# Chunked attention and four gated attention experts: turned weights of two pairs interlaced, outputs in a ring, and a new order of the steps

## The chip, the cores and the metric

The kernel runs on one core of a Trainium2 chip. The metric is the device time of one execution in microseconds (us); less is better. The cores' engines are named as the profile names them: PE (TensorE matmuls, PEld their weight loads), DVE (VectorE), ACT (ScalarE), POOL (GpSimd), SP (SyncE, which issues nearly all DMAs).

## What is computed

For 8 batches of 8 heads, 576 positions and 64 values a head: attention within chunks of 64 positions, whose output is the input x of four attention experts with a causal softmax over all 576 positions, gated by the top two of four logits.

```python
scores = np.matmul(q_c, k_c.transpose(0, 1, 2, 4, 3)) / 8      # chunks of 64
attn = np.exp(scores - scores.max(-1, keepdims=True))
attn = attn / (attn.sum(-1, keepdims=True) + 1e-09)
x = np.matmul(attn, v_c)                                       # then (B, S, H * D)
logits = x @ w_gate                                            # top 2 of E=4, softmax -> w
for e in range(E):
    q, k, v = x @ wq[e], x @ wk[e], x @ wv[e]                  # 512 -> 64
    s = np.where(causal, -1e9, q @ k.T / 8)
    a = softmax(s)
    out += mask[..., None] * w[:, :, kk:kk + 1] * (a @ v @ wo[e])
```

## The kernel before

All matmuls are float32; the projections, the expert scores and the output projection are made from three products of a high and a low half (hi·hi, hi·lo, lo·hi). The 4608 rows of x are 36 groups of 128. The work of PE is cut into 372 **steps**, in this text and in the table `ORDER` by their names:

- `as` u (L510): chunk scores of unit u (one or two groups; the first four units, 0 to 3, are one group each). DVE takes the maxima and subtracts them (L520, L522), ACT makes the exponentials (L529), DVE sums and reciprocals (L531, L533, L535), DVE (group 0) or POOL (all others) multiplies by them (L538).
- `at` u (L549): the chunk weights are turned on PE, and copied from PSUM into the tile `et` (ACT L557, and DVE L554 for half of units 0 and 1, which `FAST` names). `av` u (L570): chunk values, which ACT and DVE split into `xh` and `xl` (L592, L594).
- `m` i and `v` g (both L461, in `project`): queries and keys of a column tile, and the values and gate logits of a group. ACT and DVE split the results (L627, L632, L634; `vv` L490).
- `s` p (L712): causal scores of pair p (one batch, two experts), six steps a pair (p.1 to p.5 and p) of 64 to 448 columns, two banks each, one bank for each of the two experts. DVE evicts each bank with the mask and the row minimum (L722), ACT makes exponentials and sums (L729), POOL multiplies by reciprocal and gate (L753).
- `st` (L786): the expert weights are turned, four steps a pair; ACT copies them into the tile `aT` (L800), DVE adds three corners (L764). `o` p (L820): weights times values for the pair, read from two `aT` tiles, one for each expert; ACT and DVE split them into `uh` and `ul` (L829, L834). `w` i (L850): output projection of 128 rows, copied out by ACT or DVE (L861, L864) and stored.

The weights come in as eight transfers of 256 or 260 KB (L439), are rounded by ACT (L442) and their low halves made by POOL (L446).

The steps use PE in four **forms**: quarters of the array (`as`, `av`), halves by rows (`at`, `st`, `s`), halves by columns (`o`), and the full array (`m`, `v`, `w`).

The order on PE is the hand-written table `ORDER`. A list scheduler (`Plan`), run when the program is built, follows it with its own table of costs, and from its clock the order on the other engines results; `LATER` and `MOVED` shift their keys, `LOADS` orders the first DMAs, and `FILLS` puts idle matmuls (L892) between the first steps. A step holds tiles from pools: 8 PSUM banks (`bank`), `e` and `et` tiles for the chunk weights, two `aT` tiles, four `at` tiles of raw expert weights. A step can't be placed before every tile in its `uses` is free.

## Time and profile before

| | us |
|---|---|
| median of 3 runs | 386.6 (386.0 to 387.44) |
| the profiled execution | 386.02 |
| its span in the profile | 384.3 |
| PE busy | 374.5 (97%) |
| DVE, ACT, POOL busy | 272.1, 270.3, 170.7 |

The profile has one execution, cut by engine, by source line and by tile. PE's matmuls are pipelined and their ends are modelled, so that neighbouring rows overlap; what a step costs is read from the distance of its start to the next one's.

### The profile page before, as it was taken

How to read it: one execution, taken by the hardware profiler on the slowest of the kernel's cores; microseconds unless marked ns; L12 is line 12 of the kernel's file. 1: busy time of each engine (PE TensorE's matmuls, PEld its weight loads, DVE VectorE, ACT ScalarE, POOL GpSimd, SP SyncE). 2: the span in 40 equal slices, each digit the busy share in tenths (PEclk: the TensorE clock that was granted, in tenths of full speed). 3: DMA queues.
4: the chain of work that ended last, by engine and by line, in shares of the span. 5: the costliest groups of instructions: out<-in, count | busy, mean ns of one | idle time of the engine just before them, and what ended most of it. 6: DMA issues, size and time to landing. Idle time of an engine off the chain costs nothing.

```text
span 384.3 us, 14186 instructions
## 1 busy us (share of the span) xinstructions
PE 374.5 (97%) x5602; PEld 330.2 (86%) x5603; DVE 272.1 (71%) x946; ACT 270.3 (70%) x890; POOL 170.7 (44%) x335
## 2 busy tenths in 40 slices
PE   6799999999999999999999999999999999999996
PEld 4699999898989899797997989988989889897674
DVE  3667899999489795888436779776755766668531
ACT  3564799789746965979744496798494765969651
POOL 6653255657163069455160205763705046166700
PEclk9999999999999999999999999999999999999999
DMA  8954532605252270414106126003100110000224
GB/s 286 380 200 181 195 96 78 217 3 148 77 184 93 90 245 28 163 61 139 57 29 197 53 68 239 29 3 128 67 17 15 30 58 1 2 29 3 110 84 164
DMA packets 22098, 40.76 MB, mean 106 GB/s; under 512 B 2448, under 2 KB 2704, under 8 KB 22032
## 3 DMA queue, kind: packets, MB, share of 16 engines
q1 hardware_dynamic: 21744, 39.47, 29.8%
q8 instruction: 44, 0.72, 0.8%
q10 hardware_dynamic: 288, 0.39, 0.3%
q14 instruction: 22, 0.18, 0.1%
HBM read 30.42 MB, written 9.44 MB: 104 GB/s over the span
## 4 chain that ended last, share of the span: by engine, by line
PE 92%; DMA 3%; DVE 2%; ACT 1%; issue 1%; POOL 1%; SPq 0%; POOLq 0%
PE bank L461 39%; PE bank L850 14%; PE bank L820 12%; PE bank L712 11%; PE bank L786 6%; PE bank L570 5%; PE bank L510 4%; PE bank L549 2%; DMA at<-in_wqk_dram 2%; DMA qs<-in_qt_dram 1%; POOL e L538 1%; DVE xl L594 0%; DVE e L522 0%; DVE mx L520 0%; ACT e L529 0%
## 5 line engine op out<-in xcount | busy, mean ns | idle before, releaser
L753 POOL TENSOR_SCALAR at<-at,st,gate 128x320 f32<-128x320 f32 (+4 forms) x160 | 95.0, 611 | 74.5 <-DVE st L743 49.0
L729 ACT ACTIVATE at<-at,st 128x448 f32<-128x448 f32 (+4 forms) x160 | 90.0, 601 | 0.1
L722 DVE CUSTOM_DVE_ANT_0 at<-bank,mask 128x448 f32<-128x448 f32 (+4 forms) x160 | 60.0, 425 | 12.2 <-PE bank L712 11.4
L461 PE MATMUL bank<-xh,wqk_hi 128*128 128x384 f32 (+1 forms) x208 | 65.5, 326 | 0.0
L461 PE MATMUL bank<-xl,wqk_hi 128*128 128x384 f32 (+1 forms) x208 | 65.2, 323 | 0.0
L461 PE MATMUL bank<-xh,wqk_lo 128*128 128x384 f32 (+1 forms) x208 | 65.1, 323 | 0.0
L800 ACT ACTIVATE aT<-bank 128x128 f32<-128x128 f32 (+2 forms) x256 | 57.0, 377 | 2.4 <-PE bank L786 2.0
L538 POOL TENSOR_TENSOR e<-e,mx 128x1024 f32<-128x1024 f32 (+1 forms) x21 | 34.3, 1645 | 50.1 <-DVE mx L535 28.3
L820 PE MATMUL bank<-aT,vv 128*64 128x448 f32 (+4 forms) x384 | 46.7, 392 | 0.0
L820 PEld LDWEIGHTS bank<-aT,vv 128*64 128x64 f32 x384 | 25.0, 137 | 21.8 <-issue 15.2
L764 DVE STREAM_TRANSPOSE aT<-at 32x96 f32<-32x96 f32 x128 | 34.5, 269 | 12.5 <-POOL at L753 9.0
L461 PE MATMUL bank<-wvg_hi,xh 128*128 128x260 f32 x144 | 40.5, 288 | 0.0
L461 PE MATMUL bank<-wvg_lo,xh 128*128 128x260 f32 x144 | 39.7, 283 | 0.0
L461 PE MATMUL bank<-wvg_hi,xl 128*128 128x260 f32 x144 | 39.5, 281 | 0.0
L461 PEld LDWEIGHTS bank<-xh,wqk_hi 128*128 128x128 f32 x208 | 38.2, 188 | 0.8
L461 PEld LDWEIGHTS bank<-xl,wqk_hi 128*128 128x128 f32 x208 | 38.4, 188 | 0.5 <-DVE xl L594 0.2
L461 PEld LDWEIGHTS bank<-xh,wqk_lo 128*128 128x128 f32 x208 | 38.3, 188 | 0.0
L729 ACT ACTIVATION_READ_ACCUMULATOR at<-at,st 128x1 f32 (+1 forms) x160 | 38.1, 239 | 0.0
L712 PE MATMUL bank<-kh,qh 64*128 64x288 f32 (+4 forms) x192 | 37.1, 338 | 0.0
L490 ACT ACTIVATE vv<-bank 64x260 f32<-64x260 f32 (+1 forms) x56 | 21.6, 385 | 22.0 <-PE bank L461 21.6
L712 PE MATMUL bank<-kl,qh 64*128 64x288 f32 (+4 forms) x192 | 32.8, 294 | 0.0
L786 PEld LDWEIGHTS bank<-ident,at 64*128 64x128 f32 x704 | 28.9, 139 | 3.8 <-issue 1.5
(91 smaller groups left out, 822.4 us busy)
## 6 DMA issues: line engine op xcount, KB each, us to landing
ks<-in_kt_dram SPq DMA_DIRECT2D x36, 256.0 KB, 4.7
vs<-in_vt_dram SPq DMA_DIRECT2D x36, 256.0 KB, 4.1
qs<-in_qt_dram SPq DMA_DIRECT2D x35, 256.0 KB, 5.0
out_dram<-y SPq DMA_DIRECT2D x35, 256.0 KB, 2.0
at<-in_wqk_dram SPq DMA_DIRECT2D x4, 256.0 KB, 6.4
at<-in_wvg_dram SPq DMA_DIRECT2D x2, 260.0 KB, 4.3
at<-in_wo_dram SPq DMA_DIRECT2D x2, 256.0 KB, 5.7
qs<-in_qt_dram ACTq DMA_DIRECT2D x1, 256.0 KB, 3.6
```

The source lines that it names most:

```text
L461: pe.matmul(bk.t[:, :n_], a, x, start=(n == 0), stop=(n == 3 * KT - 1))
L490: act.activation(v_s[b].t[p0:p0 + m, j], bk.t[r0:r0 + m, 0:W_VG], AF.Copy)
L538: o = add("DVE" if u in NORM_DVE else "Pool", 0.6 if u in NORM_DVE else 0.14 + 0.87 * G, lambda: norm.tensor_tensor(e.t[:, al], e.t[:, al] ...
L712: pe.matmul(bks[s].t[:m, :w], q[own, cs], k[own, z0 + ks.start:z0 + ks.stop], start=(x == 0), stop=(x == 2))
L722: dve.tensor_tensor_reduce(out=a.t[:r, o_ + ks.start:o_ + ks.stop], in0=bk.t[:r, :w], in1=mask[:r, m0:m0 + w], scale=1.0, scalar=first, op ...
L729: act.activation(af, af, AF.Exp, scale=-1.0, bias=st.t[:r, 0, i, 0:1], accum_out=st.t[:r, 1, i, 0:1])
L753: pool.tensor_scalar(af, af, st.t[:r, 2, i, 0:1], gt.t[:r, i, e:e + 1], op0=OP.mult, op1=OP.mult)
L764: dve.transpose(dst, src)
L786: pe.transpose(bks[r].t[:, 64 * n:64 * n + 64], a.t[own, c0:c0 + 128], ident[own, own])
L800: act.activation(dst, bks[r].t[:, n:n + 64 * m].rearrange("p (j c) -> p j c", j=m), AF.Copy)
L820: pe.matmul(bk.t[64 * s:64 * s + 64, c0 - h0:h1 - h0], vs.t[:, j, 64 * (2 * pair + s):64 * (2 * pair + s) + 64], ts[s].t[:, 448 * j + c0:4 ...
L850: pe.matmul(bk.t, up[:, k, 128 * t:128 * t + 128], wp[:, k, :], start=(n == 0), stop=(n == 5))
```

## The change

- **Turned weights.** The `aT` tiles grow from 2368 to 3392 columns, and the two experts of a pair lie interlaced in one tile (`place`, with an offset table `A_OFF` for each). Two tiles so hold two pairs, where they held one.
- **Chunk weights** are turned in place: the `et` tiles are gone, `at`'s result is copied back into `e`, of which there are now three.
- **Outputs** `uh`, `ul` are a ring of 768 columns instead of 1152; where a piece wraps it is split into two (ACT 732 instructions in its order become 738, DVE 881 become 893).
- **Claims.** A step on PE claims banks (and its operands) alone; the tiles its results go to are claimed by the copies behind it. The wait of a projection for the scores that read the old queries and keys moves from the step to ACT's copy.
- **Groups 0 and 1.** The exponentials go back into the PSUM banks, DVE sums there, and DVE multiplies in two halves from PSUM into `e` (L541, L553 of the changed kernel). POOL's part in group 1 is gone.
- New planner costs, a list `EARLY` that fixes the first entries of DVE and ACT, another order of the first loads, one idle matmul between `as0` and `as1` instead of two and two new ones before `av0`, and a new `ORDER` of the same 372 steps, with new `LATER` and `MOVED`.

```diff
-TT = 448 * 4 + S
+TT = 2816 + S
-ZW = 768
+ZW = UW = 768
-A_OFF = (640, 0, 256, 768, 1280)
+A_OFF = ((640, 0, 256, 768, 1280), (1472, 1600, 1152, 576, 0))
+RAW = (768, 0)
+def place(s, j, q):
+
+    return 2816 - 576 * j + q if s else 448 * j + q
...
 ORDER = """
-as0 as1 at0 at1 av0 as3 av1 as2 v0 m1 m0 v0.1 m2 m3 v1 m3.1 m0.1 v1.1 m2.1 m1.1 at3 at2 as4 av3 av2 as5 v3 v2 m4 m6
+as0 as1 at0 at1 av0 av1 as3 m3 m0 v0 m0.1 m2 m2.1 as2 m1 m3.1 m1.1 v0.1 at3 s1.1 s0 s1 s0.1 at2 as4 av3 av2 as5 v1
...
-FILLS = {("as", 1): 2, ("at", 0): 9}
+FILLS = {("as", 1): 1, ("at", 0): 9, ("av", 0): 2}
...
-LOADS = [(x[:2], int(x[2:])) for x in "lq0 lw4 lw5 lq1 lv0 lw0 lw2 lv1 lw1 lw3 lq2 lv2 lq3 lv3 lq4 lv4".split()]
+LOADS = [(x[:2], int(x[2:])) for x in "lq0 lq1 lw4 lv0 lw5 lw0 lv1 lw2 lw1 lw3 lq2 lv2 lq3 lv3 lq4 lv4".split()]
+EARLY = [x + "@DVE" for x in ("ad0 ad0.1 ad0.2 ad0.3 ad0.4 ad0.5 ad0.6 ad0.7 ap0 ap0.1 ad1 ad1.1 ad1.2 ad1.3 ac0 ad1.4 ay0 ay0.1 ad1.5 "
+                              "ad1.6 ad1.7 ap1 ap1.1 ac1 ay1 ay1.1").split()]
+EARLY += [x + "@ACT" for x in "aa0 aa0.1 wh4 ac0 aa1 aa1.1 ax0 ax0.1 wh5 ac1 ax1 ax1.1 wh0 wh2 wh1 wh3".split()]
...
-    e_p = tiles(2, [128, 2 * H, 64], "e")
-    et_p = tiles(2, [128, 2, 512], "et")
+    e_p = tiles(3, [128, 2 * H, 64], "e")
...
-    a_p = tiles(4, [128, 1856], "at")
-    t_p = tiles(2, [128, TT], "aT")
+    a_p = [tiles(2, [128, 1856], f"at{s}") for s in range(2)]
+    t_x = tiles(2, [128, TT], "aT")
+    t_p = [list(t_x), list(t_x)]
...
-    uh = sb.tile([128, 2, 2 * S], F32R, name="uh")
+    uh = sb.tile([128, 2, UW], F32R, name="uh")
...
+        if u in FAST:
+            for s, hs in enumerate(halves):
+                o = add("ACT", act_t(64 * nh, sbuf=True), lambda s=s, hs=hs: act.activation(
+                    ps(s), e.t[:, hs], AF.Exp, scale=0.125), deps=od[s:s + 1], uses=[bq[s], e], name=("aa", u))
+                os.append(add("DVE", dve_t(64 * nh), lambda s=s, hs=hs: dve.tensor_reduce(
+                    mx.t[:, 1, hs, 0], ps(s), axis=AX.X, op=OP.add), deps=[o], uses=[bq[s], mx], name=("ad", u)))
...
+        if u in FAST:
+            od = [add("DVE", dve_t(64 * nh), lambda s=s, hs=hs: dve.tensor_tensor(
+                e.t[:, hs], ps(s), mx.t[:, 3, hs, 0:1].to_broadcast([128, nh, 64]), op=OP.mult),
+                deps=[o], uses=[bq[s], e, mx], name=("ap", u)) for s, hs in enumerate(halves)]
...
-                    et.t[:, c, 0:64 * nh], b2[c].t[:, 0:64 * nh], AF.Copy),
-                    deps=[o], uses=[b2[c], et], name=("ac", u)))
+                    et()[:, c, 0:64 * nh], b2[c].t[:, 0:64 * nh], AF.Copy),
+                    deps=[o], uses=[b2[c], e], name=("ac", u)))
...
-                po = add("PE", SCORES[w], f, deps=need, uses=bks + both, name=("s", bp), form="rows", n_ins=12.2)
+                po = add("PE", SCORES[w], f, deps=need, uses=bks, name=("s", bp), form="rows", n_ins=12.2)
...
-        o = add("PE", TURNS[half], f, deps=deps, uses=[a, t, t_s[b, e ^ 1]] + bks,
+        o = add("PE", TURNS[half], f, deps=deps, uses=[a] + bks,
...
-                                  ts[s].t[:, 448 * j + c0:448 * j + h1], start=(j == 0), stop=(j == js[-1]),
+                                  ts[s].t[:, place(s, j, c0):place(s, j, h1)], start=(j == 0), stop=(j == js[-1]),
...
+            c = (S * b + h0) % UW
+            w = min(h1 - h0, UW - c)
+            for c, p0, w in ((c, 0, w), (0, w, h1 - h0 - w))[:1 + (w < h1 - h0)]:
```

The new `ORDER` moves three things that the prediction speaks of. First PE, where the values steps stand. Before, `o3` stands alone between chunk values and a projection (the two experts' tiles are aT_105 and aT_106, and the banks are written by both in turn):

```order
L570 MATMUL bank_63<-et_84,vs_79 64x64 x2
L820 MATMUL bank_68<-aT_105,vv_99 64x128
L820 MATMUL bank_68<-aT_106,vv_99 64x128
L820 MATMUL bank_66<-aT_105,vv_99 64x448
...
L820 MATMUL bank_66<-aT_106,vv_99 64x64
L461 MATMUL bank_62<-xh_88,wqk_hi 128x384
```

In the changed kernel `o1` and `o0`, the values of two pairs (tiles aT_105 and aT_104), stand back to back:

```order
L592 MATMUL bank_67<-e_82,vs_79 64x64 x2
L838 MATMUL bank_64<-aT_105,vv_98 64x128 x2
L838 MATMUL bank_61<-aT_105,vv_98 64x448 x4
...
L838 MATMUL bank_61<-aT_105,vv_98 64x64 x2
L838 MATMUL bank_65<-aT_104,vv_98 64x128 x2
L838 MATMUL bank_66<-aT_104,vv_98 64x448 x4
...
L838 MATMUL bank_66<-aT_104,vv_98 64x64 x2
L731 MATMUL bank_63<-kh_95,qh_91 72x64
```

All sixteen values steps stand in such pairs now. Second ACT, its first entries (bank numbers with the pool's own behind them; `[waits ...]` are the semaphores of an instruction). Before:

```order
L442 ACT_TABLE_LOAD
L442 ACTIVATE wvg_hi_160<-at0_101 128x520 [waits DMAHW2_49]
L529 ACTIVATE e0_81<-e0_81 128x256 [waits DVE_49] x2
L442 ACTIVATE wvg_hi_160<-at0_101 128x520 [waits DMAHW6_49]
L529 ACTIVATE e1_82<-e1_82 128x256 [waits DVE_49] x2
L442 ACTIVATE wqk_hi_158<-at1_102 128x512 [waits DMAHW2_49]
L442 ACTIVATE wqk_hi_158<-at2_103 128x512 [waits DMAHW3_49]
L442 ACTIVATE wqk_hi_158<-at1_102 128x512 [waits DMAHW4_49]
L557 ACTIVATE et0_83<-bank4_65 128x256 [waits PE_49]
L557 ACTIVATE et1_84<-bank6_67 128x256 [waits PE_49]
```

And in the changed kernel:

```order
L539 ACT_TABLE_LOAD [waits DVE_49]
L539 ACTIVATE bank0_61<-e0_81 128x256 [waits PE_49]
L539 ACTIVATE bank1_62<-e0_81 128x256 [waits DVE_49,PE_49]
L453 ACTIVATE wqk_hi_159<-at10_102 128x512 [waits DMAHW5_49]
...
L539 ACTIVATE bank2_63<-e1_82 128x256 [waits DVE_49]
L453 ACTIVATE wqk_hi_159<-at01_101 128x512 [waits DMAHW2_49]
L579 ACTIVATE e0_81<-bank4_65 128x256 [waits DVE_49,PE_49]
L453 ACTIVATE wqk_hi_159<-at10_102 128x512 [waits DMAHW4_49]
L453 ACTIVATE wqk_hi_159<-at01_101 128x512 [waits DMAHW5_49]
L579 ACTIVATE e1_82<-bank6_67 128x256 [waits DVE_49,PE_49]
```

The first instruction was a rounding of weights and is now an exponential, so the table load stands behind DVE's first subtraction; the copy of group 1's turned weights went behind all four roundings of `wqk`, that of group 0's stands ahead of two of them. Third SP, its first DMAs. Before:

```order
L404 DMA ks_73<-in_kt_dram 128x512
L439 DMA at_101<-in_wvg_dram 128x520
L404 DMA ks_74<-in_kt_dram 128x512
L405 DMA qs_70<-in_qt_dram 128x512
L408 DMA vs_77<-in_vt_dram 128x512
L439 DMA at_101<-in_wvg_dram 128x520
L404 DMA ks_75<-in_kt_dram 128x512
L405 DMA qs_71<-in_qt_dram 128x512
L408 DMA vs_78<-in_vt_dram 128x512
L439 DMA at_102<-in_wqk_dram 128x512
L439 DMA at_103<-in_wqk_dram 128x512
L439 DMA at_102<-in_wqk_dram 128x512
```

And in the changed kernel:

```order
L414 DMA ks_73<-in_kt_dram 128x512
L414 DMA ks_74<-in_kt_dram 128x512
L415 DMA qs_70<-in_qt_dram 128x512
L418 DMA vs_77<-in_vt_dram 128x512
L450 DMA at_102<-in_wqk_dram 128x512
L450 DMA at_100<-in_wvg_dram 128x520 x2
L414 DMA ks_75<-in_kt_dram 128x512
L415 DMA qs_71<-in_qt_dram 128x512
L450 DMA at_101<-in_wqk_dram 128x512
L418 DMA vs_78<-in_vt_dram 128x512
L450 DMA at_102<-in_wqk_dram 128x512
L450 DMA at_101<-in_wqk_dram 128x512
```

Keys and queries of group 1 went ahead of the first weights, and all four `wqk` pieces stand among the first thirteen (ACT's own load of `qs` goes beside the first).

## Rows read from the trace of the kernel before

**Rows 1.** The page: busy time of the engines, and the chain's shares by engine.

```profile
PE 374.5 (97%) x5602; PEld 330.2 (86%) x5603; DVE 272.1 (71%) x946; ACT 270.3 (70%) x890; POOL 170.7 (44%) x335
...
PE 92%; DMA 3%; DVE 2%; ACT 1%; issue 1%; POOL 1%; SPq 0%; POOLq 0%
```

**Rows 2.** Timeline of PE, 0 to 17 us: start, duration, engine, line, operation; idle and releaser.

```profile
4.40 1.13 PE L510 MATMUL bank<-ks,qs 64*64 64x64 f32 x32 [1.40 <-DMA qs<-in_qt_dram]
...
6.79 1.13 PE L510 MATMUL bank<-ks,qs 64*64 64x64 f32 x32 [0.30 <-DMA qs<-in_qt_dram]
...
11.61 0.47 PE L549 MATMUL bank<-ident,e 64*128 64x64 f32 x8 [1.16 <-DVE e L538]
...
14.05 0.69 PE L570 MATMUL bank<-et,vs 64*64 64x64 f32 x32 [1.17 <-ACT et L557]
...
15.05 0.68 PE L570 MATMUL bank<-et,vs 64*64 64x64 f32 x32
15.52 0.68 PE L510 MATMUL bank<-ks,qs 64*64 64x64 f32 x32
16.13 0.74 PE L461 MATMUL bank<-wvg_hi,xh 128*128 128x260 f32 x4
```

**Rows 3.** The chain that ended last: its last piece (start, duration, what).

```profile
380.69 0.60 ACT y L861
```

**Rows 4.** Timeline of PE where its form changes, in two places.

```profile
78.12 0.28 PE L461 MATMUL bank<-wvg_hi,xl 128*128 128x260 f32 x1
78.24 0.28 PE L461 MATMUL bank<-wvg_lo,xh 128*128 128x260 f32 x1
78.45 0.40 PE L712 MATMUL bank<-kh,qh 64*128 64x288 f32 x2
...
284.17 0.50 PE L850 MATMUL bank<-wo_hi,uh 128*128 128x512 f32 x1
284.51 0.39 PE L850 MATMUL bank<-wo_hi,ul 128*128 128x512 f32 x1
284.74 0.40 PE L850 MATMUL bank<-wo_lo,uh 128*128 128x512 f32 x1
```

**Rows 5.** Timeline of PE around the largest wait behind the start.

```profile
50.00 0.27 PE L712 MATMUL bank<-kl,qh 64*128 64x192 f32 x2
50.11 0.28 PE L712 MATMUL bank<-kh,ql 64*128 64x192 f32 x2
50.56 0.71 PE L549 MATMUL bank<-ident,e 64*128 64x64 f32 x16 [0.17 <-POOL e L538]
```

**Rows 6.** Timeline of DVE and ACT, 0 to 18 us.

```profile
6.24 0.74 DVE L522 TENSOR_TENSOR e<-bank,mx 128x256 f32<-128x256 f32 x2
...
10.78 0.68 DVE L538 TENSOR_TENSOR e<-e,mx 128x512 f32<-128x512 f32 x1
...
1.23 1.28 ACT L442 ACT_TABLE_LOAD   x1 [1.23 <-PEq L922]
4.93 0.64 ACT L442 ACTIVATE wvg_hi<-at 128x520 fp32r<-128x520 f32 x1 [2.42 <-DMA at<-in_wvg_dram]
6.68 0.75 ACT L529 ACTIVATE e<-e 128x256 f32<-128x256 f32 x2 [1.11 <-DVE e L522]
```

**Rows 7.** The chain: the transfer of the 13th piece of input, and the rounding behind it.

```profile
6.68 6.40 DMA at<-in_wqk_dram
13.10 0.63 ACT wqk_hi L442
```

**Rows 8.** A block of ten score steps: PE's last, DVE's first and last evictions, and busy time.

```profile
84.81 0.51 PE L712 MATMUL bank<-kh,qh 64*128 64x448 f32 x2
...
79.16 0.46 DVE L722 CUSTOM_DVE_ANT_0 at<-bank,mask 128x288 f32<-128x288 f32 x1 [0.57 <-PE bank L712]
...
86.90 0.62 DVE L722 CUSTOM_DVE_ANT_0 at<-bank,mask 128x448 f32<-128x448 f32 x1
...
78.45:85.64 7.19, 7.19 (x129) 6.84 (x128) 6.55 (x33) 6.95 (x26) 4.07 (x12) 1.00 0.01 3
```

More of the change, by code (lines that the diff above doesn't have):

```diff
@@ L163, in fetched, with fits @@
             return stall
+        def fits(o):
+            need = {}
+            for u in o.uses:
+                if u.t is None:
+                    need[id(u.pool)] = (u.pool, need.get(id(u.pool), (None, 0))[1] + 1)
+            return all(len(p) >= n for p, n in need.values())
         order, free_t = self.rank(), {}
@@ L173, in emit @@
                 if held and eng == "DVE":
-                    if free_at["Pool"] > now or any(a.ready <= now for a in avail["Pool"]):
+                    if free_at["Pool"] > now or any(a.ready <= now and fits(a) for a in avail["Pool"]):
                         continue
@@ L194, in emit @@
                         continue
[L195 to L199 removed]
+                    if not fits(o):
                         continue
@@ L525, in stage_a @@
-        al = slice(0, 2 * nh)
-        os = []
-        for hs, need in ([(slice(0, nh), od[:1]), (slice(nh, 2 * nh), od[1:])] if u in FAST else [(al, od)]):
-            n = 64 * (hs.stop - hs.start)
-            o = add("ACT", act_t(n, sbuf=True), lambda hs=hs: act.activation(e.t[:, hs], e.t[:, hs], AF.Exp, scale=0.125),
-                    deps=need, uses=[e], name=("aa", u))
-            os.append(add("DVE", dve_t(n), lambda hs=hs: dve.tensor_reduce(
-                mx.t[:, 1, hs, 0], e.t[:, hs], axis=AX.X, op=OP.add), deps=[o], uses=[e, mx], name=("ad", u)))
+        al, halves = slice(0, 2 * nh), [slice(0, nh), slice(nh, 2 * nh)]
@@ new lines, in stage_a @@
+        if u in FAST:
+            for s, hs in enumerate(halves):
+                o = add("ACT", act_t(64 * nh, sbuf=True), lambda s=s, hs=hs: act.activation(
+                    ps(s), e.t[:, hs], AF.Exp, scale=0.125), deps=od[s:s + 1], uses=[bq[s], e], name=("aa", u))
+                os.append(add("DVE", dve_t(64 * nh), lambda s=s, hs=hs: dve.tensor_reduce(
+                    mx.t[:, 1, hs, 0], ps(s), axis=AX.X, op=OP.add), deps=[o], uses=[bq[s], mx], name=("ad", u)))
+        else:
+            o = add("ACT", act_t(128 * nh, sbuf=True), lambda: act.activation(e.t[:, al], e.t[:, al], AF.Exp, scale=0.125),
+                    deps=od, uses=[e], name=("aa", u))
+            os.append(add("DVE", dve_t(128 * nh), lambda: dve.tensor_reduce(
+                mx.t[:, 1, al, 0], e.t[:, al], axis=AX.X, op=OP.add), deps=[o], uses=[e, mx], name=("ad", u)))
@@ L549, in f @@
                     pe.transpose(b2[c].t[:, 64 * m:64 * m + 64], ef[own, 128 * m:128 * m + 128], ident[own, own])
-        o = add("PE", 0.01 + 0.243 * G, f, deps=[o], uses=[e, et] + b2, name=("at", u), form="rows", n_ins=16 * G + 0.3)
+        o = add("PE", 0.245 * G, f, deps=od, uses=[e] + b2, name=("at", u), form="rows", n_ins=16 * G + 0.3)
         od = []
@@ L627, in f @@
                 act.activation(dst(hi), src(), AF.Copy, scale=-0.125 if m < 2 else 1.0)
-            o1 = add("ACT", act_t(w_), f, deps=[o], uses=[bk], name=("za", i))
+            o1 = add("ACT", act_t(w_), f, deps=[o] + old, uses=[bk], name=("za", i))
             def f(src=src, dst=dst):
@@ L731, in scores @@
                 eo.append(add("ACT", act_t(n, 2), f, deps=[done[s]], uses=[a, st], name=("sa", bp)))
-        t_s.update({(b, 2 * pair + s): Slot(t_p) for s in range(2)})
+        t_s.update({(b, 2 * pair + s): Slot(t_p[s]) for s in range(2)})
         for s, (a, st, eo) in enumerate(parts):
```

197 lines of the change are left out of this document (96 added, 101 removed), and 53 rows, old and new, of the table MOVED.

## The prediction

> **What bounds the kernel now.** I read the page first [rows 1]: PE is busy for 374.5 of 384.3 us, the next engine, DVE, for 272.1, and the chain that ended last is 92% PE. PE's order is a fixed table, so the span is the sum of the steps' own times plus what PE loses between them. Three places can lose time, and I looked at each in its own view.
>
> The first is the start. PE's timeline [rows 2] has real work from 4.40 us, then waits for keys, queries, the softmax of groups 0 and 1 and the copies of their turned weights; the first projection starts at 16.13. Between 4.40 and 16.13 stand only eight small steps of 0.5 to 1.1 us: this stretch hangs on other engines. The second is the end: PE's last matmul is followed by a copy of 0.60 us [rows 3] and the store to 384.3, and since the last steps are output projections in both orders, I cost the end at nothing.
>
> The third is the middle, 16.13 to 380.69. There PE has no idle of any size. The largest single wait is at 50.56 [rows 5]: the two matmuls at 50.00 took 0.11 until the next start, those at 50.11 took 0.45, of which idle shows 0.17; a change of form explains some 0.1, so about 0.3 was waiting. Comparing starts of equal steps in this way I estimate some 5 us in about 50 such waits, most of them 0.05 to 0.2, this one the largest. The rest is loss where the array's form changes [rows 4]: from 78.24 to 78.45 is 0.21, where the matmul before it took 0.12 (78.12 to 78.24), so leaving the full form costs 0.09; the first full-form matmul behind values steps takes 0.34 (284.17 to 284.51), the second 0.23, so entering it costs 0.11. Between other forms the same comparison gives entries down to 0.05. One change of form is therefore 0.14 to 0.20, and at most 0.26 in the slowest kind.
>
> A profile's time is 386.02 against a span of 384.3; the median of the three runs is 386.6. I work against 386.02 and add 0.6 at the end. The smallest difference that a measurement of this kernel can tell from none is about 0.5%, 1.9 us.
>
> **The change, part by part.**
>
> *Form changes.* The arithmetic of the 372 steps is the same, so their own times cancel. Counted along PE's order of both programs, the form changes 78 times before and 67 times after. The largest single share is the values steps: with two pairs' turned weights held at once, all sixteen stand in eight pairs, which the order shows, and each pair saves a change in and out. Changes from column form to full fall from 12 to 1, from full to rows from 20 to 17, from quarters to columns from 7 to 2; against that quarters to full rise from 8 to 13. Eleven at 0.17 (the middle of 0.14 to 0.20) is -1.9 us; the ends are -1.5 (0.14 each) and -2.9 (0.26 each).
>
> *Waits in the middle.* With claims on banks alone and two pairs in flight, the order can put more work between a producer and its user. Counted in PE work by the durations of the rows, the median distance from scores to their turning rises from 14.9 to 26.8 us, from turning to values from 3.0 to 5.8, from chunk scores to their turning from 12 to 19. So waits on late data, like the one of [rows 5], should shrink, while those for the second of two banks still being evicted stay. The bounds are the 5 us above, of which at most 3 are of the first kind, and new waits at other places: -3.0 to +2.0. I take -0.8, nearer to nothing than to -3, since the row nearest to it shows that even the largest is 0.3.
>
> *The start.* The fourth piece of input is now all that `as1` needs. The second had landed when `as0` began at 4.40 [rows 2] and the 13th at 13.08 (6.68 + 6.40, [rows 7]), 0.79 apart on average, so the fourth lands at about 6.0 and `as1` starts near 6.1 instead of 6.79. But ACT's table load, which ran at 1.23 for 1.28 us while ACT had nothing else to do [rows 6], now waits for DVE's first subtraction. That ends near 6.65 (6.24 plus half of the two, 0.74), so the first exponential starts at about 7.95 instead of 6.68. Two exponentials (0.75) to 8.70; two sums from PSUM, three interposed operations of group 1 at some 0.35 each, two small ones, and the halves of the norm at 0.35 each (the pair of such operations at 6.24 took 0.74) bring `at0` to about 11.1, against 11.61 before: earlier, since the 0.68 norm at 10.78 is halved and POOL is out of it. Group 1's chain lies behind it on DVE, so `at1` comes at about 13.3, and `av0` stands behind `at1` in the order. The copy of group 1's turned weights then stands on ACT behind all four roundings of `wqk`, the last of which is the 14th piece: 13.08 + 0.7 lands, + 0.63 rounded [rows 7], so the copy starts at about 14.4, `av1` at 14.8, the copies of x (0.66) end near 16.1, and the first projection starts near 16.2. Before it started at 16.13 with `as2` done, now `as2` is still to come: 0.47 (15.05 to 15.52, an equal step) plus the 0.07. So +0.6. The lower end is 0.0, if the pieces land 0.04 closer together than that mean (0.04 x 12 = 0.5). The upper end is 1.45, which a rival below works out. The idle matmuls before `as1` and `av0` fill waits only.
>
> [...] [Rows 6] show the load at 1.28 us, and behind it no delay, but the next instruction there waited for a transfer until 4.93 [rows 6], so a delay would have been hidden. [...]
>
> *The rest.* Six more instructions on ACT, twelve on DVE from the split outputs: 18 at under 0.3 us on engines at 70%, hidden by PE, unless they fall into a block of scores (below). Copying the turned chunk weights in place costs nothing in itself; POOL loses one norm.
>
> Sum: -1.9 - 0.8 + 0.6 = **-2.1 us**, 383.9 for a run like the profiled one, **384.5** for the median.
>
> **The rivals.**
>
> *A larger gain.* The late-data waits go nearly whole (-3.0) and the start is even: 386.6 - 1.9 - 3.0 = 381.7. For it speaks the near doubling of all three distances, against it that most waits are on banks, which no distance helps.
>
> *The start eats the gain.* If the first exponential is later than the 1.28 us of the load by as much again (a rival that needs no page: any start-up of the exponential behind the load that [rows 6] hide), `at1` comes near 14.6, `av1` near 15.5, the projection at 17.0, with `as2` to come: +1.45 instead of +0.6, and with middle waits at -0.3, 386.6 - 1.9 - 0.3 + 1.45 = 385.9. [...]
>
> *Slower: blocks of scores bound by DVE.* The new order has four blocks of 11 or 12 score steps, with only turnings between them; before, the longest had ten. In that one [rows 8] PE went through in 7.19 us and DVE was busy for 6.55 of them, and DVE fell behind: its first eviction started 0.71 after the first score (78.45 to 79.16), the tenth 2.09 after its own (84.81 to 86.90). A step's two evictions take about 0.86 (79.16 to 86.90 is nine steps), so 2.09 us are five banks; six, or 2.6 us, is where PE waits, since two of eight are being written. Two steps more at this rate add 0.3, which just stays below. If another DVE job falls between (the splits of 0.4 to 0.7 us, or the new pieces of the outputs), each of the four blocks overruns by 1 to 2 us. With 1.3 each: 386.6 - 2.1 + 5.2 = 389.7. Against it: DVE's lag here included gating work of 0.4 us and PE still lost nothing.
>
> *The change doesn't do what it says*, for instance interlaced tiles that still wait for one another: then 386.6. The order shows pairs of values steps, and their semaphores name no wait of one pair's copies for the other's, so this has little.
>
> **How the numbers follow.** My forecast, 382.7 to 386 with its likeliest value at 384.5, has 0.53, of which I put 0.32 below 384.7 (0.5% under the median) and 0.21 above. The larger gain has 0.18, the eaten gain 0.14, the blocks 0.12, no effect 0.03. Faster by over 0.5%: 0.32 + 0.18 = 0.50; within 0.5%: 0.21 + 0.14 + 0.03 = 0.38; slower: 0.12. The range leaves out the blocks and the far side of the larger gain: 381.5 to 387.2, the upper end being the worse start with new waits of 1 us in the middle (386.6 - 1.9 + 1.0 + 1.45).
>
> **What would show it.** Right: values steps in pairs 2.85 apart with nothing between; first exponential near 7.95 with the table load before it; first projection near 16.2; from there to PE's last matmul 362.3 us (364.5 before, less 2.7, and `as2`'s 0.5). Wrong: idle on PE at a score behind DVE's evictions, or an `o` or `st` that waits for ACT or POOL for over 0.3 us; or a first projection behind 17. A granted clock below 1.00 in the start would overthrow every duration above.

## The result: 0.65% slower, and the profile after

The median went from 387.02 us (386.00 to 387.95, 6 runs) to **389.65 us** (388.63 to 389.85, 6 runs): ratio 1.0065, 95% interval 1.0043 to 1.0087. The forecast was 384.5, with a range up to 387.2. The profiled execution took 389.57 us against 386.02, 3.55 more; its span is 387.9.

The page of the changed kernel, the two lines that answer to [rows 1]:

```profile
PE 377.6 (97%) x5602; PEld 333.2 (86%) x5604; DVE 274.4 (71%) x957; ACT 270.5 (70%) x898; POOL 169.9 (44%) x336
...
PE 95%; DMA 2%; ACT 1%; DVE 1%; issue 1%; POOL 0%; SPq 0%; ACTq 0%; POOLq 0%
```

Nothing in these says where 3.5 us went: the engines' shares are those of before, and the chain is a little more PE (95% instead of 92%). The timeline of PE at the start does. It answers to [rows 2] (start, duration, engine, line, operation; idle and releaser):

```profile
4.39 1.13 PE L521 MATMUL bank<-ks,qs 64*64 64x64 f32 x32 [1.39 <-DMA qs<-in_qt_dram]
5.99 1.14 PE L521 MATMUL bank<-ks,qs 64*64 64x64 f32 x32 [0.47 <-DMA qs<-in_qt_dram]
7.06 3.38 PE L915 MATMUL bank<-y 128*128 128x512 bf16 x9
10.87 0.58 PE L571 MATMUL bank<-ident,e 64*128 64x64 f32 x8 [0.43 <-POOL wqk_lo L457]
13.53 0.69 PE L571 MATMUL bank<-ident,e 64*128 64x64 f32 x8 [2.08 <-DVE e L553]
14.55 0.63 PE L915 MATMUL bank<-y 128*128 128x512 bf16 x1 [0.33 <-issue]
15.12 1.99 PE L592 MATMUL bank<-e,vs 64*64 64x64 f32 x64
16.88 1.08 PE L521 MATMUL bank<-ks,qs 64*64 64x64 f32 x32
```

`as1` at 5.99, `at0` at 10.87 and `at1` at 13.53 are close to the 6.1, 11.1 and 13.3 forecast. But between `at0` and `at1` PE idles 2.08 us, and from then on each step takes longer by half or more: the 32 matmuls of `as3` take 1.08 us where equal ones took 0.68 [rows 2]. The windows of PE name the reason (busy time, then the granted clock, DMA share and GB/s):

```profile
12.00:13.00 1.00, 0.00 (x0) 1.00 1.08 414
13.00:14.00 1.00, 0.47 (x8) 0.53 1.05 391
14.00:15.00 1.00, 0.67 (x7) 0.50 1.04 379
...
19.00:20.00 1.00, 1.00 (x7) 0.55 1.04 385
20.00:21.00 1.00, 1.00 (x10) 1.00 1.06 387
```

The granted clock fell to 0.50 at 13.07 us, 1.6 us into the idle stretch, and came back at 19.90. In the profiled execution of before it stayed at 1.00 from the first record of the clock at 8.85 us on. (Ahead of its first record, at 9.66 us in the changed kernel, the column says 1.00 without one; the last section comes back to this.)

ACT's first instructions answer to [rows 6] and [rows 7]:

```profile
6.72 1.28 ACT L539 ACT_TABLE_LOAD   x1 [6.72 <-DVE e L534]
8.02 0.69 ACT L539 ACTIVATE bank<-e 128x256 f32<-128x256 f32 x2
...
12.58 0.63 ACT L453 ACTIVATE wqk_hi<-at 128x512 fp32r<-128x512 f32 x1 [1.40 <-DMA at<-in_wqk_dram]
13.12 0.37 ACT L579 ACTIVATE e<-bank 128x256 f32<-128x256 f32 x1
13.94 1.31 ACT L453 ACTIVATE wqk_hi<-at 128x512 fp32r<-128x512 f32 x2 [0.46 <-DMA at<-in_wqk_dram]
15.15 0.37 ACT L579 ACTIVATE e<-bank 128x256 f32<-128x256 f32 x1
```

The table load does stand behind DVE's subtraction, and the first exponential starts at 8.02, 0.02 us behind its end.

To add up, I cut both timelines at `at3`, which by then has the same work behind it but for `v1` (there in before, later in the changed kernel):

| | before | changed | difference |
|---|---|---|---|
| start to `at3`, `v1` left out | 23.48 | 26.96 | **+3.48** |
| `at3` to the last matmul, `v1` left out | 355.73 | 355.70 | **0.0** |
| `v1` | 1.44 | 1.53 | +0.1 |
| last copy and store | 3.62 | 3.66 | 0.0 |

So the start lost 3.5 us where +0.6 was forecast, and the middle gained nothing where 2.7 was. For the middle I compared each step's distance to the next with the fast fifth of its kind between the same neighbours, over both traces. These floors sum to 346.8 and 345.4: **-1.4**, the changes of form. What lies above them grew by **+1.4**: waits over 0.1 us are 28 with 5.5 us, 13 with 2.3 before. This split is an estimate: with the neighbours grouped more coarsely or more finely, the floors differ by 0.8 to 2.2 us, and the rest by as much the other way; its sign stays. The values steps show the gain (two steps, 48 matmuls, from 86.54 to 92.09: 2.78 each, 2.85 for one that stands alone, the median of before's sixteen):

```profile
86.54 5.62 PE L838 MATMUL bank<-aT,vv 128*64 128x128 f32 x48
92.09 0.25 PE L731 MATMUL bank<-kh,qh 64*72 64x64 f32 x2
```

And two places show what took it back. In the timeline of PE and ACT, a score of 448 columns takes 1.23 us (77.95 to 79.18), 0.69 being usual: a bank it writes came free only with the last of 14 copies of turned weights on ACT, at 78.23.

```profile
77.95 0.81 PE L731 MATMUL bank<-kh,qh 64*128 64x448 f32 x2
78.29 0.66 PE L731 MATMUL bank<-kl,qh 64*128 64x448 f32 x2
...
79.18 0.34 PE L805 MATMUL bank<-ident,at 64*128 64x64 f32 x4
...
75.11 3.12 ACT L819 ACTIVATE aT<-bank 128x128 f32<-128x128 f32 x14
```

And inside step `v21` PE stands still in the middle of a projection, with nothing to wait for in the program ("issue"):

```profile
237.93 0.28 PE L472 MATMUL bank<-wvg_hi,xl 128*128 128x260 f32 x1
238.61 0.28 PE L472 MATMUL bank<-wvg_lo,xh 128*128 128x260 f32 x1 [0.40 <-issue]
```

0.68 from start to start where 0.12 is usual: 0.56 us of standstill.

Over all 118 runs of the kernel before that were timed beside the experiments, the granted clock of the whole execution is 1.000 or 0.999 in 61 (median 386.20 us), 0.996 in 54 (median 387.65) and lower in three, so the kernel before itself falls now and then into what the changed kernel always shows (0.989 to 0.996).

### The profile page after: what moved, and what is told of

The parts are those of the page before. It is cut to its first block, busy times and chain, and to the rows that moved or that the text cites. A ratio compares the mean times of both kernels' runs of the same rounds, so it can differ in the third digit from the quotient of the medians.

```text
span 387.9 us, 14196 instructions
## 1 busy us (share of the span) xinstructions
PE 377.6 (97%) x5602; PEld 333.2 (86%) x5604; DVE 274.4 (71%) x957; ACT 270.5 (70%) x898; POOL 169.9 (44%) x336
## 4 chain that ended last, share of the span: by engine, by line
PE 95%; DMA 2%; ACT 1%; DVE 1%; issue 1%; POOL 0%; SPq 0%; ACTq 0%; POOLq 0%
PE bank L472 40%; PE bank L873 13%; PE bank L731 11%; PE bank L838 11%; PE bank L805 6%; PE bank L592 5%; PE bank L521 5%; PE bank L571 2%; DMA at<-in_wqk_dram 2%; POOL wvg_lo L457 0%; ACT at L750 0%; ACT y L884 0%; SPq L414 0%; DVE e L553 0%; DVE y L887 0%
## 5 line engine op out<-in xcount | busy, mean ns | idle before, releaser
L774 POOL TENSOR_SCALAR at<-at,st,gate 64x64 f32<-64x64 f32 (+4 forms) x160 | 95.0, 613 | 35.0 <-DVE st L764 22.8
L750 ACT ACTIVATE at<-at,st 128x320 f32<-128x320 f32 (+4 forms) x160 | 88.9, 573 | 0.6 <-DVE st L743 0.4
L472 PE MATMUL bank<-xh,wqk_hi 128*128 128x384 f32 (+1 forms) x208 | 66.3, 330 | 0.0
L743 DVE CUSTOM_DVE_ANT_0 at<-bank,mask 128x320 f32<-128x320 f32 (+4 forms) x160 | 59.6, 424 | 8.8 <-PE bank L731 7.3
L557 POOL TENSOR_TENSOR e<-e,mx 128x1024 f32<-128x1024 f32 (+1 forms) x20 | 33.1, 1658 | 40.7 <-DVE mx L550 36.4
L838 PE MATMUL bank<-aT,vv 128*64 128x448 f32 (+4 forms) x384 | 45.0, 390 | 0.0
L681 POOL TENSOR_TENSOR gs<-vv,gs 128x20 f32<-128x20 f32 x8 | 2.3, 292 | 92.9 <-DVE gs L675 92.9
L472 PEld LDWEIGHTS bank<-xh,wqk_hi 128*128 128x128 f32 x208 | 39.0, 193 | 0.7
L750 ACT ACTIVATION_READ_ACCUMULATOR at<-at,st 128x1 f32 (+1 forms) x160 | 33.8, 211 | 0.0
```

The costliest lines, as they stand in the source:

```text
L472: pe.matmul(bk.t[:, :n_], a, x, start=(n == 0), stop=(n == 3 * KT - 1))
L557: od = [add("Pool", 0.14 + 0.87 * G, lambda: pool.tensor_tensor(e.t[:, al], e.t[:, al], mx.t[:, 3, al, 0:1].to_broadcast([128, 2 * nh, 64] ...
L743: dve.tensor_tensor_reduce(out=a.t[:r, o_ + ks.start:o_ + ks.stop], in0=bk.t[:r, :w], in1=mask[:r, m0:m0 + w], scale=1.0, scalar=first, op ...
L750: act.activation(af, af, AF.Exp, scale=-1.0, bias=st.t[:r, 0, i, 0:1], accum_out=st.t[:r, 1, i, 0:1])
L774: pool.tensor_scalar(af, af, st.t[:r, 2, i, 0:1], gt.t[:r, i, e:e + 1], op0=OP.mult, op1=OP.mult)
L838: pe.matmul(bk.t[64 * s:64 * s + 64, c0 - h0:h1 - h0], vs.t[:, j, 64 * (2 * pair + s):64 * (2 * pair + s) + 64], ts[s].t[:, place(s, j, c0 ...
```

## The experiments

Each run was timed against the kernel before on the same chip. Two theories stood at the outset: **A**, the idle gap between `at0` and `at1` lets PE's clock fall, and that is what the time went to; **B**, ACT's table load and the chain behind it are late, and the clock is a bystander. In the middle a third, **C**, joined them: PE waits for its own instructions.

**Is the clock the cause, or a bystander?** Eight idle matmuls between `at0` and `at1`:

```diff
-FILLS = {("as", 1): 1, ("at", 0): 9, ("av", 0): 2}
+FILLS = {("as", 1): 1, ("at", 0): 9, ("at", 1): 8, ("av", 0): 2}
```

> The changed kernel with eight idle matmuls more, put between at0 and at1, where PE idled 2.08 us before its granted clock fell to 0.50 (13.2 to 19.95 us). Theory A, the idle gap lets the clock fall and the half clock costs most of the start's loss: the clock stays at 1.00, the first projection starts near 16.5 instead of 17.89, and the time falls by about 2.4 us to 387.2. Theory B, the start is late because of the table load behind DVE's subtraction and the copies behind the roundings, and the clock is a bystander: the first projection still starts behind 17.5 and the time stays within 0.5 us of 389.6.

389.87 us, ratio 1.0072 (1.0040 to 1.0104): no faster, though the clock stayed at 1.00 in the profiled execution and at 0.998 or more in all others but one (0.994). By its time theory A had fallen; by its trace it had not. `at3`'s start came 1.56 us earlier (25.40), but the middle had grown by 1.8 us. The scheduler, with more work on PE, had put out another order on DVE, ACT and POOL in places, a stall of 0.7 stood inside `v22`, and one wait of 1.3 us (to 110.12) is put down to ACT, whose copy had ended 0.7 us before: by what is shown further down, this is a stall of the same kind.

The early table load:

```diff
             (nc.sync if g else nc.scalar).dma_start(q_s[g].t, qt[g])
+            if g == 0:
+                act.activation(early, early, AF.Exp)
```

> The changed kernel with one exponential of a single column on ACT right behind its first DMA issue, so that the table load runs before 3 us and not at 6.72. Theory A: at0 and at1 come some 1.2 us earlier but the gap between them stays near 2 us, the clock still falls to 0.50, and the time stays within 0.7 us of 389.6. Theory B: the first exponential starts near 6.7, everything behind it follows, and the time falls by 1.2 us or more, to 388.4 or less.

388.58 us, 1.0040 (1.0023 to 1.0057): 1.1 better than the changed kernel's 389.65, more than A allowed (0.7) and 0.2 short of what B asked for. But `at1` didn't move (13.52 against 13.53); only `at0` came earlier (9.83), so the gap grew to 3.11 us, the clock fell all the same, and came back earlier (0.74 mean in 18 to 19 us, 0.50 there in the changed kernel). The gain is 0.9 us in the start, `at3` at 26.04. So the table load does cost about a microsecond here.

Both together:

> The changed kernel with both: idle matmuls between at0 and at1, and the early table load. Theory A: as with the idle matmuls alone or up to 0.7 us less, 386.5 to 387.2, since the copy of group 1 still stands behind the rounding of the 14th piece. Theory B: the same as with the early table load alone, 388.4.

388.71 us, 1.0034 (1.0017 to 1.0050): near B's number, not A's. The start was the shortest so far, 25.33, but the middle 0.9 longer, with stalls of 0.5 inside `v3` and 0.8 inside `v22`.

And the kernel before with a gap, three idle matmuls fewer ahead of `at0`:

```diff
-FILLS = {("as", 1): 2, ("at", 0): 9}
+FILLS = {("as", 1): 2, ("at", 0): 6}
```

> The kernel before with six idle matmuls instead of nine between as1 and at0, so that PE idles about 2.0 us there instead of 1.16. Theory A: the clock falls in this kernel too, for some microseconds behind the gap, and the time rises by 2 to 3 us over the kernel before. Theory B: only idle matmuls are gone, the clock stays at 1.00 and the time is that of the kernel before within 0.5 us.

387.60 us against 387.44, ratio 1.0021 (0.9999 to 1.0042): by its time B, since the 2 to 3 us of A didn't come. In its profile, though, the clock does fall; windows of PE (busy time, clock, DMA share, GB/s):

```profile
13.00:14.00 1.00, 0.12 (x4) 0.95 1.07 408
14.00:15.00 1.00, 0.95 (x36) 0.50 1.04 393
...
16.00:17.00 1.00, 1.00 (x52) 0.50 1.06 383
17.00:18.00 1.00, 1.00 (x32) 0.85 1.04 383
```

The start grew by 1.4 us (24.88), the middle not at all (355.54). The granted clock of the whole execution is below 0.998 in 11 of 12, in the runs of the kernel before beside it in 21 of 30; the ratio is small because of these, in which a fall costs 387.65 - 386.20 = 1.45. (No such execution of the kernel before was profiled; that it falls in the start follows from `e11` below, where filling the start ends it.) The gaps are no longer than those of [rows 2] (1.11, 0.35 and 0.92 us in this profile): what is missing is the work of three idle matmuls ahead of them. So the clock falls here without a gap of 2 us, and the kernel before stands close to it.

**The clock without its side effects.** `e1` had moved other engines. Here the idle matmuls stand inside `at1`'s own step, into a bank it holds anyway, and no instruction of another engine changes place (first line). The second run adds an order in which `as2` stands ahead of the first projections; the third prices a change of form, by one matmul of 16 columns on the full array (two records in the profile) between the two values steps of each pair; the fourth fills the kernel before in the same way.

```diff
+            for _ in range({1: 7}.get(u, 0)):
+                pe.matmul(b2[0].t, warm[:, 0:128], warm, start=True, stop=True)
...
-as0 as1 at0 at1 av0 av1 as3 m3 m0 v0 m0.1 m2 m2.1 as2 m1
+as0 as1 at0 at1 av0 as3 av1 as2 m3 m0 v0 m0.1 m2 m2.1 m1
...
+            if bp in SECOND:
+                pe.matmul(parts[0][2].t[:, 0:16], ident, ident[:, 0:16], start=True, stop=True)
...
+            for _ in range({0: 4}.get(u, 0)):
+                pe.matmul(b2[0].t, warm[:, 0:128], warm, start=True, stop=True)
```

> The changed kernel with seven idle matmuls issued inside step at1, into the bank that at1 is about to write, so that they wait for nothing and no other engine's order moves (in the first run with idle matmuls the order of DVE and ACT moved in the middle and some idle matmuls waited for ACT). Theory A (the clock): the clock stays at 1.00, the first projection starts near 16.6 instead of 17.89, the stretch from at3 on keeps its 355.7 us, and the time falls by 2.0 to 2.9 us to 386.8 to 387.6. Theory B (the clock is a bystander): within 0.7 us of 389.6 as with the idle matmuls of the first run.

389.07 us, 1.0062 (1.0040 to 1.0085). By the time it is B again. By the trace the clock is at 1.00 and `at3` at 25.43 against 26.96: **1.53 us back in the start**, as A says, and lost again in the middle (357.34, 1.64 more), though nothing but seven idle matmuls at 12 us had changed. The loss has two addresses: `v3`, where 0.53 us is lost at 44.58, and `v22`, where PE stands still with every operand there (1.79 between two starts):

```profile
236.13 0.28 PE L472 MATMUL bank<-wvg_hi,xh 128*128 128x260 f32 x1
237.92 0.28 PE L472 MATMUL bank<-wvg_hi,xl 128*128 128x260 f32 x1 [1.51 <-issue]
```

> The same with the chunk scores of groups 2 and 3 moved back to where the kernel before had them, as3 ahead of av1 and as2 ahead of the first projection. If what is left of the start's loss at full clock is that these steps stand behind the first projection where PE no longer waits, the start shortens by 0.5 to 1.0 us more against the run with idle matmuls inside at1. Rival: the copies of x are what the first projection waits for and as2 only delays it: no gain, or up to 0.5 us slower.

388.95 us, 1.0055 (1.0036 to 1.0073). The start shrank by another 0.58 (24.85), and a standstill of 1.28 us stood inside `v22`.

> The run with idle matmuls inside at1, and one matmul of 16 columns in the full form more, ahead of the second values step of each of the eight pairs, which breaks the pairs' common form and moves no other engine's order. If a change of form costs what the prediction took (0.17, two changes each, and the matmul itself some 0.05), 16 x 0.17 + 8 x 0.05 = 3.1 us more than without; if the pairs gain nothing because the forms cost nothing there, 0.4 us more.

394.33 us, 1.0187 (1.0161 to 1.0213). Two values steps with the small matmul between them:

```profile
84.39 2.92 PE L843 MATMUL bank<-aT,vv 128*64 128x128 f32 x24
87.24 0.40 PE L837 MATMUL bank<-ident 128*128 128x16 f32 x2
87.56 2.92 PE L843 MATMUL bank<-aT,vv 128*64 128x128 f32 x24
90.42 0.25 PE L734 MATMUL bank<-kh,qh 64*72 64x64 f32 x2
```

6.03 us, 5.55 in the changed kernel: 0.48 for the matmul and two changes of form, 3.8 over the eight pairs; the middle grew by 3.6 (360.98 against 357.34), of which 0.3 are standstills. A change of form has the price I gave it or a little more. What a pair itself shows is less: 5.55 against 5.70 for two steps that stand alone, 1.2 us over eight pairs. The price is that of the profiled executions, which differ by 3.0 us (392.66 and 389.68); the medians differ by 5.3, and what the slower executions of `e7` lost isn't in the trace.

> The kernel before with four idle matmuls inside at0 and four inside av0, in the two stretches where PE idles 1.16 and 1.17 us. Theory A: of the executions of the kernel before those with a mean clock of 0.996 (387.2 to 388.2) are executions in which the clock fell in the start, those with 1.000 (385.7 to 386.8) are those in which it did not; with the idle matmuls all are at 1.000, and the median falls by 0.7 to 1.2 us to 386.2 or so. Theory B: no change, 387.4 within 0.4.

387.32 against 386.48, 1.0016 (1.0001 to 1.0031). The clock held in all executions (0.998 or more), but idle matmuls of this size push `at0` and `av0` back (24.29 against 23.48), and a standstill of 0.59 us appeared inside `v14`.

**What the standstill is.** In the changed kernel it comes at the 18th matmul counted from the start of `v22`, which the order puts ahead of `v21`. With 7 matmuls added ahead of it (`e5`) it comes at the 11th, with 15 (`e7`: 7 and four small ones of two records each) at the 3rd. It is bound to a count of PE's instructions, not to a step or an operand. And it stands in a burst of input transfers:

```profile
226.00:234.00 8.00, 8.00 (x164) 1.00 0.01 3
234.00:240.00 6.00, 5.60 (x164) 1.00 0.84 266
```

These are windows of the changed kernel (PE's busy time, clock, DMA share, GB/s). Its page lists a DMA queue that is neither input nor output, and two packets of it fall into the burst from 234 to 240 us:

```profile
q8 instruction: 44, 0.72, 0.7%
...
q1 hardware_dynamic: 859, 1.57, 81.7%
q8 instruction: 2, 0.03, 2.2%
```

(A second queue of that kind, q14, has 22 packets and 0.18 MB.) PE has 5602 matmuls and 5604 weight loads, so one packet of q8 comes for about 255 of them, and the standstills of `e5` in `v3` and `v22` lie 3164 matmuls and 25 packets apart, 127 matmuls for each.

Hence theory C, an inference from these counts: the packets (0.72 MB in 44, 16 KB each) bring PE's next block of instructions, and where a block's border falls into a burst of loads, it is late. It can be tested by taking out as many of the warming matmuls ahead of the first step as were added later: the same count, so the border is back at its place; or by other counts, so that it moves out of the burst.

```diff
-    for _ in range(64 if banks else 0):
+    for _ in range(57 if banks else 0):
```

57 with `e5`'s fill, 50 with `e6`'s, 56 with `e8`'s:

> The seven idle matmuls inside at1 again, and seven of the 64 warming matmuls at the very start taken out, so that every later PE instruction has the same count ahead of it as in the changed kernel. In the runs with added idle matmuls PE stood still inside steps v22 or v21, with no wait in the program, always the same number of instructions from the start (seven matmuls earlier in the step order where seven had been added), for 0.4 to 1.7 us. Theory C: PE's instructions come in blocks, and a block that is asked for while input loads fill the DMA engines arrives late; added instructions moved its border to an earlier time and so ate what the clock gave back. Then here the stall is back at v21 with about 0.5 us or up to 1.5 more for the earlier clock time, the stretch from at3 on is 355.7 to 357.0, and the time falls to 387.6 to 388.6. Rival: the stall belongs to the idle matmuls themselves or to chance: 389.1 as before.

387.88 us, 1.0036 (1.0015 to 1.0057), in C's range. The standstill is back in `v21`, at the same matmul as in the changed kernel:

```profile
236.15 0.28 PE L472 MATMUL bank<-wvg_hi,xl 128*128 128x260 f32 x1
236.98 0.28 PE L472 MATMUL bank<-wvg_lo,xh 128*128 128x260 f32 x1 [0.55 <-issue]
```

The middle is 355.87, 1.47 less than in `e5` from seven warming matmuls. And now the clock's price can be read with equally many instructions: with the clock at 1.00 (in the profiled execution; three of the 12 are at 0.996), `at3` stands at 25.13, **1.8 us** ahead of the changed kernel. One profile of each run carries this: in `e5` and `e7`, which are the same program up to there, `at3` stands at 25.43 and 24.75, so the price is 1.5 to 2.2.

> The order of the start as in the second last run but one (as3 ahead of av1, as2 ahead of the first projection), seven idle matmuls inside at1, and 14 of the 64 warming matmuls taken out, so that the border of the block lies seven matmuls later than in the changed kernel, near the end of v21. Theory C: the stall there shrinks by 0.8 us or vanishes, the first projection starts near 17.0 with as2 done, and the time is 386.9 to 387.7, unless another border now falls into a burst of loads. Rival (the stall is chance): 388.9 as the run with this order.

387.14 us against 386.81, 1.0001 (0.9984 to 1.0018). Of the standstill 0.14 us is left, at the 25th matmul (236.93 to 237.19, 0.12 being usual), seven places further as C asks; the old place now:

```profile
235.37 0.28 PE L472 MATMUL bank<-wvg_hi,xl 128*128 128x260 f32 x1
235.49 0.28 PE L472 MATMUL bank<-wvg_lo,xh 128*128 128x260 f32 x1
```

The middle is 355.33, 1.43 less than in `e6`. The start is another matter: `e6`'s order gained 0.58 against `e5`, but 0.09 here against `e9` (25.04), and the first projection stands at 17.66 where about 17.0 was expected.

The packets themselves speak for C. In nine traces PE loses 0.4 us or more at a time in the middle without a missing operand, 13 times in all, and each of these standstills ends 1.30 to 1.56 us behind the end of a packet of q8: in the changed kernel the packet ends at 237.27 and PE goes on at 238.61, in `e5` 236.55 and 237.92, in `e9` 235.46 and 236.98. `e1`'s wait for ACT is one of them (108.72 and 110.12), and so is what is left in `e10` (235.88 and 237.19). In the 2 us around each the DMA engines are busy for 74% or more.

> The kernel before with four idle matmuls inside at0 and four inside av0, and eight warming matmuls less. Theory C: the stall of 0.6 us inside v14 that the run without the compensation had is gone, and the clock is at 1.00 in all executions: 386.2 to 386.5, none above 387.2. Rival: 387.3 as in the run without the compensation.

386.65 us, 0.9997 (0.9980 to 1.0014): a little above C's 386.2 to 386.5, with two executions above 387.2. The clock is at 0.998 or more in all of them, there is no standstill, the start is 24.40 and the middle 355.58. So the kernel before can be made steady, but not faster: what the fill costs is what the falls cost on average.

**Can the changed order beat before?** Three more starts: with the early table load of `e2`, `v0` and its group ahead of the other projections, and 10 idle matmuls inside `at1` (47 warming ones); then with the roundings of two pieces of `wvg` behind group 1's exponentials on ACT, and of two pieces of `wqk` behind the copies of x; then with fewer idle matmuls (55 warming ones, the same count in all).

```diff
-as0 as1 at0 at1 av0 as3 av1 as2 m3 m0 v0 m0.1 m2 m2.1 m1 m3.1 m1.1 v0.1 at3
+as0 as1 at0 at1 av0 as3 av1 as2 v0 m3 m0 v0.1 m3.1 m2 m0.1 m1 m2.1 m1.1 at3
...
+        for x, y in (("wh2", "ax1.1"), ("wh1", "ax1.1"), ("wh4", "aa1.1"), ("wh5", "aa1.1")):
+            named[y + "@ACT"].after.append(named[x + "@ACT"])
+            named[x + "@ACT"].left += 1
...
-FILLS = {("as", 1): 1, ("at", 0): 9, ("av", 0): 2}
+FILLS = {("as", 1): 1, ("at", 0): 5, ("av", 0): 2}
-            for _ in range({1: 10}.get(u, 0)):
+            for _ in range({1: 6}.get(u, 0)):
```

> The changed kernel with the early table load, ten idle matmuls inside at1, 17 warming matmuls less (the border of the instruction block where the last run but one had it), and the order of the start changed: as3 ahead of av1, as2 ahead of the first projection, and v0, which needs the x of group 0 alone, as the first projection. Theory D: what is left of the start's loss at full clock (1.5 us) is the order there: a first projection that needs both groups' x, with as2 behind it. Then it starts near 16.5 with as2 done, and the time falls from 387.1 by 0.5 us or more, to 386.6 or less. Rival E: the copies on ACT set the end of the start: group 1's turned weights are copied behind all four roundings, and all copies of x behind that; then the order alone changes nothing, 387.1 within 0.4.

386.86 us, 1.0007 (0.9994 to 1.0019), 0.3 below `e10`: rival E by the number. `at3` is at 24.90, the middle 355.44. The first projection is at 17.61, not near 16.5, behind an `as2` that waits for its queries:

```profile
15.95 0.69 PE L598 MATMUL bank<-e,vs 64*64 64x64 f32 x32 [0.42 <-ACT e L585]
16.98 0.70 PE L525 MATMUL bank<-ks,qs 64*64 64x64 f32 x32 [0.34 <-DMA qs<-in_qt_dram]
17.61 0.75 PE L476 MATMUL bank<-wvg_hi,xh 128*128 128x260 f32 x4
```

> The same, with ACT's order in the start changed too: the roundings of two pieces of wvg behind the first exponentials of group 1, and those of the last two pieces of wqk behind the copies of x. Rival E: at1 comes near 12.8 instead of 13.5 to 14.0, av1 near 14.5, the first projection near 15.7 with as2 done, and the time falls by 0.8 us or more against the run without this, to 386.2 or less, which is below the kernel before. Theory D: no further gain, within 0.3 us of the run without this.

387.00 us, 1.0012 (0.9998 to 1.0026): D by the number. A miss for E: `at0` (11.41) and `at1` (14.07) now stand behind the idle matmuls, which nothing in the program waits for:

```profile
7.51 3.97 PE L924 MATMUL bank<-y 128*128 128x512 bf16 x9
11.41 0.46 PE L580 MATMUL bank<-ident,e 64*128 64x64 f32 x8
```

> The last run with five idle matmuls instead of nine ahead of at0, six instead of ten inside at1, and eight warming matmuls more (the same count of instructions in all). In the last run at0 started at 11.41 though its weights were normed at 10.2, and at1 at 14.07 though normed at 13.0: the idle matmuls stood in their way, nine of them in 3.97 us. Theory E (ACT's copies and, in the last run, the idle matmuls set the end of the start): at0 starts near 10.3, at1 near 13.1, the first projection near 16.0, and the time falls by 0.7 us or more to 386.3 or less, which would be a little below the kernel before. Rival: the clock falls again as PE idles 1 to 1.5 us in both places, or the transfers set the end: 387.0 or more.

387.64 us, 1.0020 (1.0004 to 1.0036): the rival's number, with the clock at 1.00. `at0` at 10.38 and `at1` at 13.49, and still `as2` at 16.43 waits 0.36 for the transfer of `qs`, and the first projection starts at 17.06, no earlier than in `e13` (17.03). Neither ACT's order nor the fill sets the start then; what is left to set it is the new order of the loads, in which `as2`'s keys and queries come 16th and 17th (14th and 15th before). That is argued from this wait; an earlier load wasn't tried. Six of the 12 executions took 387.5 to 388.1 us with the clock at 0.998 or more, five 386.8 to 387.1; the profile is of a short one, so what the others lost isn't shown.

No version beats the kernel before; `e10` to `e13` are level with it, and none reaches the 386.20 of its executions in which the clock holds.

## Why the prediction was wrong

- **The start, +0.6: the step that failed.** The times of the steps were right up to `at1` (6.1, 11.1 and 13.3 forecast; 5.99, 10.87 and 13.53 measured), and the table load came as foreseen: first exponential 8.02, 7.95 forecast. What failed is the sentence that put everything behind `at1` at durations of [rows 2], taken at a clock of 1.00. The forecast's own numbers held the warning: `at0` at 11.1 and `at1` at 13.3, with 0.47 of work in between [rows 2], leave some 1.7 us of idle, longer than any gap of [rows 2] from there on (1.17), and the idle matmuls, counted as "fill waits only", left just this gap open. That the profiled execution of before held a clock of 1.00 hid that about half of the others fall. Measured: +3.48, of it 1.8 for the clock (`e9`; 1.5 to 2.2 by `e5` and `e7`). The sign named for it, a first projection behind 17, came at 17.89. The other 1.65 are at full clock: about 0.65 from a first projection at 16.78 instead of 16.13 (forecast 0.07), about 0.6 for `as2`, now behind it (forecast 0.47), and a rest of 0.4 that I can't place. These shares are read from one profile each, and putting `as2` back ahead in `e10` gave 0.09, since it then waits for its queries; the cause of the 1.65 stays open.
- **Form changes, -1.9: right in kind, -1.4 by the floors (0.8 to 2.2 by other groupings).** `e7` confirms the price of the largest kind (0.48 for an insert with two changes).
- **Waits in the middle, -0.8: wrong in sign, +1.4 by the same floors.** 0.56 of it is the standstill, of which nothing was known. The rest, some 0.85, are short waits; the one looked at, the score at 77.95, is for a bank that ACT frees late. The longer distances between producer and user that I counted on don't touch a wait for a bank, as the prediction said, and the new order has more short waits; that they are all of this kind isn't shown. Which of them could be won back wasn't tried. With the standstill moved out (`e10`, `e12` to `e14`), the middle is 355.3 to 355.6 against 355.73: the whole gain of the change is 0.2 to 0.4 us, and the start costs more.
- **The slower rival, 389.7: right time, other mechanism.** Blocks of scores bound by DVE would show score steps waiting for evictions; the view of PE's waits lists no score step of the changed kernel that waits for DVE. It is no credit that the time fell there.
- **The start eats the gain: not by that way.** The rival wanted a start-up behind the table load, with `at1` near 14.6. No run shows such a start-up, and its length, "as much again" as the load, was the author's assumption: here, where ACT was idle until the load at 6.72, the load took 1.28 us, the exponential came 0.02 us behind it, and `at1` at 13.53.
- **The clock.** The prediction's last sentence, that a clock below 1.00 in the start would overthrow every duration, is what happened. It stood as a caveat and should have been a rival with a price.

## What to carry to other kernels

Where an order is changed at the start, list PE's idle gaps in the new order beside those of the old one, and give any that is longer than what the trace shows at full clock a rival in which what is behind it runs at the 0.50 seen here. Look at the granted clock of many executions before calling a start undisturbed (the kernel before was below 0.998 in 57 of 118). And when an edit worth 1.5 us in one place moves nothing in the total, look for a standstill with "issue" as its releaser: here 0.56 us became 1.67 with seven matmuls more ahead of it (`e5`) and 0.14 with seven fewer (`e10`), so compare differences under 2 us at the same instruction count. And look at the times of the packets of the queue that the page calls instruction, here q8: each standstill ended 1.30 to 1.56 us behind one.

## What the runs showed of the hardware

- In a stretch of 2.08 us of PE idle (11.45 to 13.53) the granted clock fell to 0.50 at 13.07 and stayed there until 19.90, while PE was busy for 6.1 of the 7 us from 13 to 20; with the gap filled (`e1`, `e3`, `e5` to `e7`, `e9`, `e12`, `e13`) the windows of PE show 1.00 throughout the start. In `e2`, a gap of 3.11 us, it fell later (15.10) and came back earlier (18.51). In `e4` it fell (13.90 to 17.31) with no gap over 1.11 us. Price: 1.4 us in the kernel before, 1.5 to 2.2 in the changed one.
- PE stood still for 0.4 to 1.7 us at a fixed count of its instructions, where that fell into a burst of loads (DMA engines busy for 74% or more in the 2 us around), and for 0.14 us with the count shifted by seven; it went on 1.30 to 1.56 us behind the end of a packet of the instruction queue q8 (44 packets, 0.72 MB, 16 KB each). That these packets bring PE's instructions is inferred from their count and times.
- The column of the granted clock doesn't cover the first 8 to 11 us. Nine idle matmuls take 2.58 us before, 3.38 in the changed kernel and 3.97 in `e13`, and the windows of PE from 9 to 10 us say 1.00 in all three (before, changed, `e13`):

```profile
9.00:10.00 1.00, 1.00 (x6) 1.00 1.07 381
...
9.00:10.00 1.00, 1.00 (x4) 1.00 1.04 392
...
9.00:10.00 1.00, 1.00 (x3) 1.00 1.04 384
```

The traces' first record of the clock is at 8.85 us before, 9.66 in the changed kernel and 11.29 in `e13`, and 8.07 to 11.00 in the other runs. In the changed kernel the idle matmuls start 0.43 us apart ahead of it (9.17, 9.59) and 0.22 behind it (9.85, 10.06), in the kernel before likewise (8.26, 8.69; 9.20, 9.42). `as0` and `as1` ahead of it take 1.13 and 1.14 us in the changed kernel, nearer to the 1.08 of `as3` at a recorded 0.50 than to the 0.68 of an equal step at 1.00 [rows 2]. From this I infer that PE worked at about half its later pace until then, and that the 1.00 that the windows give there stands for no record. So equal matmuls have to be compared in that stretch, and idle matmuls at that pace can delay the steps they were to bridge: in `e13`, whose first record comes last, nine took 3.97 us, and `at0` (11.41) and `at1` (14.07) stood behind the idle matmuls.
